# A linear-attention and expert kernel: key tiles in pairs, with copies and sums first, y steps from a list, and block sums on GpSimd

## The chip, the cores and the metric

The kernel runs on one core of one Trainium2 chip. The time is device microseconds of one execution, from launch to end as the device reports it; the median of several runs is given, and one further execution was recorded by the profiler. Engines carry the profile's names: PE (TensorE matmul) and PEld (its weight load), DVE (VectorE), ACT (ScalarE), POOL (GpSimd), and SP, which here only issues DMAs.

## The reference

For 2048 tokens of width 512 the reference mixes an attention block without softmax and a mixture of eight experts, of which all eight are used:

```python
qkv = (x @ wqkv)                                  # 32 heads of 16
phi = lambda t: where(t > 0, t + 1, exp(t)) + 1e-6
kv  = einsum("bhsd,bhse->bhde", phi(k), v)
z   = einsum("bhsd->bhd", phi(k))
a   = (phi(q) @ kv / (phi(q) @ z + 1e-6)) @ wo
logits = x @ w_gate                               # 8 experts, top 8
b   = sum over e of softmax(logits)[e] * (silu(x @ w1[e]) @ w2[e])
g   = sigmoid(sum(x * gate_w))
out = g * a + (1 - g) * b
```

All of it is in float32.

## The kernel before

Each float32 operand is split into a high part in the rounded format fp32r and a low part with the remainder, and each product is made of three matmuls (high by high, high by low, low by high: `mm3`, lines 59 to 62). A split is a copy by ACT and a subtraction by DVE (`split`, lines 350 to 352). Large products are done with a scheme of seven block products in place of eight (P1 to P7), for which sums and differences of blocks of the operands are needed.

The program has three stages, written out in the order in which each engine's queue takes the instructions; no scheduler changes that order. The first stage works on keys, the second and third on experts and queries. The change lies in the first, the function `keys`, up to about 130 us of the span.

Tokens are in four blocks of 512 (ORD = 2, 3, 0, 1), each of four tiles of 128. For blocks 2 and 3 `g_proj` makes the key projection of one tile directly, in two groups of columns (g = 0 and 1, 12 matmuls each), and `group_done` and `pk_done` put phi on it: ACT takes the exponential (line 74) and the relu (line 75) of the bank, DVE the minimum and sum (line 78), ACT the high part `pkh` (line 65, by the helper `act_copy`) and DVE the low part (line 88). GpSimd adds the tile into `pks` by an accumulating DMA (lines 472 and 477). `split_xt` splits the tokens by rows, and `y_acc` then adds x^T phi(k) of that tile to four banks that stay through the stage: 12 matmuls over 512 columns, or 6 for half of them with `part` 0 or 1.

Blocks 0 (A) and 1 (B) are done as pairs j = 0 to 3: tile j of A on top and tile j of B at the bottom. `x_sum` makes the sums of the token blocks (four steps for the keys, p = 0, and four for blocks 2 and 3, p = 1, which the experts use), `w_sums` those of the key weights, `x_part` and `w_part` split them. `pair` issues seven products into PSUM banks: product 0 into bank a; a copy of bank a goes into bank b (ACT, kb<-ka), on which product 2 is added; product 1 goes into bank c, which is copied to s3; product 3 is added to a, then copied to s2; product 4 is added to c, and DVE adds it to s2 (line 689); product 5 is added to a, and DVE adds it to s3 (line 696); product 6 is added to a. `late` keeps the second halves of phi until `flush` issues them. `more` lists what other work stands between the products (`extra(0)` to `extra(3)`), and the loop at lines 720 to 741 places the y steps of the tiles before. There is one bank b and one bank c, and there are two of a.

The SP queue issues the loads in program order: `load_xt` for rows of tokens (two rooms), `load_x` for columns (three rooms), and later the first expert weights (`m.load`).

Of the kernel before, what the change touches and what calls it, by code (L numbers as in the profile page):

```python
# [26 lines left out]
NTT = TB // P  # L27
# [5 lines left out]
HALF = 2 * P  # L33
# [290 lines left out]
def keys(m):  # L324
# [195 lines left out]
    def x_sum(p, step):  # L520
        a, b = raw[2 * p], raw[2 * p + 1]
        b11, b21, b12, b22 = a[:, :2], a[:, 2:], b[:, :2], b[:, 2:]
        dst, x, y = ((b11, b12, b11), (b12, b22, b12), (b22, b22, b11), (b21, b21, b22))[step]
        v.tensor_sub(dst, x, y)

    def x_part(p, i):
        a, b = raw[2 * p], raw[2 * p + 1]
# [26 lines left out]
            nc.sync.dma_start(w0[i], src[:, 2 * i:2 * i + 2, :HALF])  # L554

    def w_sums():
        v.tensor_add(w11, w10, w11)
        v.tensor_sub(w10, w00, w10)
        v.tensor_sub(w00, w11, w00)
        v.tensor_sub(w01, w01, w00)  # L560

    def w_part(i):
        src = {1: w11, 5: w10, 3: w00, 4: w01}[i]
# [33 lines left out]
    for t in range(NTT - 1):  # L597
# [4 lines left out]
    x_keep(0, (2, 0)), x_keep(2, (2, 1))  # L602


    A, B = ORD[2], ORD[3]
    beside = {
        0: (lambda: w_sums(), lambda: w_part(1), lambda: split_x(A, 0)),
        1: (lambda: split_x(A, 1), lambda: split_x(A, 2), lambda: split_x(A, 3), lambda: w_part(4)),
        2: (lambda: x_sum(0, 0), lambda: split_x(B, 2), lambda: split_x(B, 3), lambda: x_part(0, 1)),
        3: (lambda: x_sum(0, 1), lambda: x_sum(0, 2), lambda: x_part(0, 3)),  # L610
    }
    T1 = ORD[1] * NTT
    for t in range(NTT):
        for g in range(2):
            g_proj(T1 + t, g, alone=True)
        split_xt(T1 + t)
        y_acc(T1 + t - 1)
        for do in beside[t]:
            do()
        if t == 1:  # L620
            x_keep(4, (3, 1))
            load_xt(A)
            band(mask.rearrange("p (b e) -> p b e", e=DH), [[-DH, P // DH], [0, DH]], 1)
# [21 lines left out]

    late = []

    def flush():
        while late:
            late.pop(0)()  # L650

    def group(t, g, src, done):
        d = pk[t][0]
        if g == 0:
            act_copy(lg[:, t, :E + 2], src[:, HALF:W[0]])
        dst, src = d[:, HALF:] if g == 0 else d[:, :HALF], src[:, :HALF]
        m.phi_first(dst, src)
        late.append(lambda: m.phi_last(dst, src))
        if done:
            late.append(lambda: pk_done(t, False))  # L660


    def pair(j, extra):
        top, bot = A * NTT + j, B * NTT + j
        a = m.ps_tile(f"ka{j}", "a")
        product(j, 0, a, True)
        flush()
        b = m.ps_tile(f"kb{j}", "b")
        act_copy(b[:, :W[0]], a[:, :W[0]])
        yield  # L670
        c = m.ps_tile(f"kc{j}", "c")
        product(j, 1, c, True)
        s3 = oh_tile(f"k3_{j}")[:, :HALF]
        act_copy(s3, c[:, :HALF])
        yield
# [20 lines left out]
        v.tensor_add(s3, a[:, :HALF], s3)  # L696
        group(bot, 1, s3, True)
        yield
        product(j, 6, a, False)
        flush()  # L700
# [2 lines left out]
    def last_step(run):  # L703
        for _ in run:
            pass

    more = {
        0: ((lambda: w_part(3),), (lambda: w_part(5), lambda: x_part(0, 5)),
            (lambda: split_xt(4), lambda: x_sum(0, 3)), (lambda: x_part(0, 6), lambda: split_xt(0), lambda: load_x(3))),
        1: ((), (lambda: split_xt(5),), (lambda: x_sum(1, 0), lambda: x_part(1, 1)),  # L710
            (lambda: split_xt(1), lambda: x_sum(1, 1))),
        2: ((lambda: split_xt(6, True),), (lambda: x_part(1, 5), lambda: split_xt(2, True)),
            (lambda: x_sum(1, 2), lambda: split_xt(7, True)),
            (lambda: split_xt(3, True), lambda: m.load(0), lambda: m.load(1))),
        3: ((lambda: x_part(1, 3),), (lambda: x_sum(1, 3),), (lambda: x_part(1, 6),), (lambda: m.prep(0, 0),)),
    }

    old = None
    touch()
    for j in range(NTT):  # L720
        before = (B * NTT + j - 1, A * NTT + j - 1) if j else (T1 + NTT - 1, None)
# [11 lines left out]
        next(run)  # L733
        y_acc(before[0], 1)
        next(run)
        if j and j < NTT - 1:
            y_acc(before[1], 0)
        next(run)
        if j:
            y_acc(before[1], 1 if j < NTT - 1 else None)  # L740
# [746 lines left out]
```

## Time and profile before

| | |
|---|---|
| Median of 3 runs | 2351.36 us (2350.36 to 2353.77) |
| The profiled execution, its own time | 2351.11 us |
| Its span, first to last instruction | 2349.4 us |
| Busy: PE, DVE, ACT, POOL | 2320.7, 1835.6, 1416.9, 158.0 us |
| Mean granted TensorE clock | 0.993 of full speed |

All rows of the profile count from the start of the span. A row of the timeline gives start, duration, engine, line, operation, the output and input names and, in brackets, how long the engine stood idle before and what released it. Starts on one engine can overlap the end of the instruction before, since engines pipeline. Waits are listed as total, number of times and longest.

### The profile page before, as it was taken

Reading aid. Unit: us, or ns where it says so; the run is one execution under the profiler, and the core shown is the slowest. Engines: PE = TensorE matmul, PEld = TensorE weight load, DVE = VectorE, ACT = ScalarE, POOL = GpSimd, SP = SyncE. Lnnn points to the kernel's source line nnn. Section 1 sums busy time; section 2 is a strip of 40 time slices with the busy share of each in tenths; the row PEclk is TensorE's granted clock in tenths of the full one; section 3 lists DMA queues with packets and bytes.
Section 4 is the critical chain, followed back from the end, with each engine's and each line's share of the span. In section 5 each row is a group of like instructions: output and inputs, shape, how many; then the busy total and the mean of one; then the engine's idle time right before and its main releaser. Section 6 shows DMA issues by size and latency. Waiting matters only on the chain.

```text
span 2349.4 us, 31599 instructions
## 1 busy us (share of the span) xinstructions
PE 2320.7 (99%) x10523; PEld 1924.3 (82%) x10523; DVE 1835.6 (78%) x3132; ACT 1416.9 (60%) x2686; POOL 158.0 (7%) x218
## 2 busy tenths in 40 slices
PE   9799999999999999999999999999999999999999
PEld 8678888888888888888888888888888888888887
DVE  6589888888888888888766868777677776867777
ACT  6477766666665666666555656555565655655553
POOL 1010100000000000000001000000011101000011
PEclk9899999999999999999999999999999999999999
DMA  8379888888889888888946444574556646466568
GB/s 273 110 245 308 286 269 257 273 265 270 273 259 282 260 265 268 272 281 250 318 156 174 150 157 161 171 206 139 161 175 184 184 148 179 153 175 174 162 213 234
DMA packets 323908, 513.42 MB, mean 219 GB/s; under 512 B 52176, under 2 KB 220512, under 8 KB 323104
## 3 DMA queue, kind: packets, MB, share of 16 engines
q1 hardware_dynamic: 294832, 465.14, 59.7%
q0 software_dynamic: 23200, 45.21, 11.0%
q8 instruction: 82, 1.34, 0.2%
q10 hardware_dynamic: 5712, 1.06, 0.2%
q14 instruction: 82, 0.67, 0.1%
HBM read 345.03 MB, written 163.13 MB: 216 GB/s over the span
## 4 chain that ended last, share of the span: by engine, by line
PE 95%; ACT 0%; DVE 0%; issue 0%
PE p L60 15%; PE p L62 15%; PE p L61 15%; PE a L60 9%; PE a L62 9%; PE a L61 9%; PE c L60 4%; PE c L62 4%; PE c L61 4%; PE b L62 2%; PE b L61 2%; PE b L60 2%; PE s L60 0%; PE s L62 0%; PE s L61 0%; PE y L60 0%
## 5 line engine op out<-in xcount | busy, mean ns | idle before, releaser
L60 PE MATMUL p<-ho,w 128*128 128x512 f32 x1602 | 623.3, 389 | 0.0
L62 PE MATMUL p<-ho,w 128*128 128x512 f32 x1602 | 623.2, 389 | 0.0
L61 PE MATMUL p<-ho,w 128*128 128x512 f32 x1602 | 623.2, 389 | 0.0
L959 DVE TENSOR_TENSOR ho<-s,ho 128x512 fp32r<-128x512 f32 x784 | 538.3, 687 | 39.4 <-ACT ho L65 36.8
L65 ACT ACTIVATE ho<-s 128x512 fp32r<-128x512 f32 x784 | 482.0, 622 | 16.6 <-PE p L62 10.8
L60 PEld LDWEIGHTS p<-ho,w 128*128 128x128 f32 x1602 | 300.8, 188 | 62.8 <-DMA w<-w2stash 0.5
L62 PEld LDWEIGHTS p<-ho,w 128*128 128x128 f32 x1602 | 300.8, 188 | 62.3
L61 PEld LDWEIGHTS p<-ho,w 128*128 128x128 f32 x1602 | 300.8, 188 | 62.3
L65 ACT ACTIVATE o<-rs 128x512 fp32r<-128x512 f32 x224 | 129.4, 578 | 203.0 <-PE c L62 113.6
L65 ACT ACTIVATE o<-rm 128x512 fp32r<-128x512 f32 x240 | 138.8, 578 | 144.0 <-PE a L62 66.0
L885 DVE TENSOR_TENSOR s<-c,s 128x512 f32<-128x512 f32 x116 | 80.2, 691 | 153.5 <-PE c L62 145.4
L65 ACT ACTIVATE ws<-rm 128x256 fp32r<-128x256 f32 (+1 forms) x204 | 114.9, 572 | 48.3 <-DMA w2stash<-ws 44.3
L797 ACT ACTIVATE s<-s 128x512 f32<-128x512 f32 x224 | 138.5, 618 | 6.2 <-DVE s L890 3.4
L797 ACT ACTIVATE s<-b 128x512 f32<-128x512 f32 x112 | 67.2, 600 | 103.3 <-PE b L62 98.0
L205 DVE TENSOR_TENSOR o<-rm,o 128x512 fp32r<-128x512 f32 x180 | 123.3, 685 | 1.3 <-ACT o L65 1.2
L65 ACT ACTIVATE s<-a 128x512 f32<-128x512 f32 x116 | 69.3, 597 | 89.4 <-PE a L62 89.3
L219 DVE TENSOR_TENSOR ws<-rm,ws 128x512 fp32r<-128x512 f32 x155 | 106.6, 688 | 17.2 <-ACT ws L65 16.2
L890 DVE TENSOR_TENSOR s<-a,s 128x512 f32<-128x512 f32 x116 | 79.8, 688 | 51.1 <-PE a L62 50.8
L205 DVE TENSOR_TENSOR o<-rs,o 128x512 fp32r<-128x512 f32 x168 | 114.4, 681 | 5.6 <-ACT o L65 5.6
L65 ACT ACTIVATE b<-a 128x512 f32<-128x512 f32 x116 | 67.2, 579 | 60.9 <-PE a L62 60.8
L1018 POOL DMA_DIRECT2D acct<-c x30 | 25.8, 859 | 914.4 <-DVE c L1012 747.7
L65 ACT ACTIVATE s<-c 128x512 f32<-128x512 f32 x116 | 68.9, 594 | 22.2 <-PE c L62 22.2
(371 smaller groups left out, 4581.6 us busy)
## 6 DMA issues: line engine op xcount, KB each, us to landing
w<-w2stash SPq DMA_DIRECT2D x403, 512.0 KB, 4.1
w2stash<-ws SPq DMA_DIRECT2D x359, 256.0 KB, 4.6
rm<-wm SPq DMA_DIRECT2D x228, 256.0 KB, 5.2
rs<-wm SPq DMA_DIRECT2D x108, 256.0 KB, 4.0
wb<-wgtd SPq DMA_DIRECT2D x16, 512.0 KB, 5.0
acct<-c POOLq DMA_DIRECT2D x30, 256.0 KB, 6.2
acct<-d POOLq DMA_DIRECT2D x30, 256.0 KB, 5.3
acct<-k POOLq DMA_DIRECT2D x30, 256.0 KB, 5.0
```

What stands on the lines that cost most here:

```text
L60: nc.tensor.matmul(ps, wh, xh, start=start, stop=False, skip_group_check=True)
L61: nc.tensor.matmul(ps, wh, xl, start=False, stop=False, skip_group_check=True)
L62: nc.tensor.matmul(ps, wlo, xh, start=False, stop=stop, skip_group_check=True)
L65: nc.scalar.activation(dst, src, AF.Copy, scale=scale, bias=bias)
L205: v.tensor_sub(two(o, 1), src, f32(two(o, 0)))
L219: v.tensor_sub(two(w, 1), src, f32(two(w, 0)))
L797: nc.scalar.activation(dst, src, AF.Silu)
L885: v.tensor_add(sn[g, 2], bank[g, "c"], sn[g, 2])
L890: v.tensor_add(sn[g, 3], bank[g, "a"], sn[g, 3])
L959: v.tensor_sub(h[1], s, f32(h[0]))
L1018: nc.gpsimd.dma_start(m.acct[part.h, j, dt], s, accum_op=ALU.add)
```

## The change

In `pair`, the copy of bank a to bank b and the other bank copies and sums now stand ahead of `flush` or right behind the product that they need, and `extra` is called at other places. The y steps are taken in halves from a list `behind`, to which each finished tile adds two; `y_next` takes one from its front. The token sums and the weight sums are done by GpSimd in place of VectorE, and the first of them, with two splits, are issued ahead of the tiles of block 3. The lists `beside` and `more` are dealt out anew.

```diff
     def x_sum(p, step):
...
-        v.tensor_sub(dst, x, y)
+        nc.gpsimd.tensor_sub(dst, x, y)
...
     def w_sums():
-        v.tensor_add(w11, w10, w11)
-        v.tensor_sub(w10, w00, w10)
-        v.tensor_sub(w00, w11, w00)
-        v.tensor_sub(w01, w01, w00)
+        nc.gpsimd.tensor_add(w11, w10, w11)
+        nc.gpsimd.tensor_sub(w10, w00, w10)
+        nc.gpsimd.tensor_sub(w00, w11, w00)
+        nc.gpsimd.tensor_sub(w01, w01, w00)
...
+    behind = []
+    def y_next():
+        if behind:
+            y_acc(*behind.pop(0))
     A, B = ORD[2], ORD[3]
+    split_x(A, 0), split_x(A, 1)
+    w_sums()
+    x_sum(0, 0), x_sum(0, 1)
     beside = {
-        0: (lambda: w_sums(), lambda: w_part(1), lambda: split_x(A, 0)),
-        1: (lambda: split_x(A, 1), lambda: split_x(A, 2), lambda: split_x(A, 3), lambda: w_part(4)),
-        2: (lambda: x_sum(0, 0), lambda: split_x(B, 2), lambda: split_x(B, 3), lambda: x_part(0, 1)),
-        3: (lambda: x_sum(0, 1), lambda: x_sum(0, 2), lambda: x_part(0, 3)),
+        0: (lambda: split_x(B, 2), lambda: split_x(B, 3), lambda: w_part(1)),
+        1: (lambda: x_sum(0, 2), lambda: split_x(A, 2), lambda: split_x(A, 3), lambda: w_part(4)),
+        2: (lambda: x_sum(0, 3), lambda: x_part(0, 1), lambda: w_part(3)),
+        3: (lambda: x_part(0, 3),),
     }
...
         split_xt(T1 + t)
-        y_acc(T1 + t - 1)
+        y_next() if t else y_acc(T0 + NTT - 1)
+        behind.extend(((T1 + t, 0), (T1 + t, 1)))
...
     def pair(j, extra):
         product(j, 0, a, True)
-        flush()
         b = m.ps_tile(f"kb{j}", "b")
         act_copy(b[:, :W[0]], a[:, :W[0]])
+        flush()
+        extra(0)
         yield
         product(j, 1, c, True)
         act_copy(s3, c[:, :HALF])
+        extra(1)
         yield
         product(j, 2, b, False)
-        extra(0)
...
         product(j, 3, a, False)
+        flush()
         act_copy(s2, a[:, :W[0]])
-        flush()
-        extra(1)
+        extra(2)
         yield
         product(j, 4, c, False)
-        extra(2)
         v.tensor_add(s2, c[:, :W[0]], s2)
...
         product(j, 5, a, False)
+        v.tensor_add(s3, a[:, :HALF], s3)
         flush()
+        group(bot, 1, s3, True)
         extra(3)
-        v.tensor_add(s3, a[:, :HALF], s3)
-        group(bot, 1, s3, True)
...
     more = {
-        0: ((lambda: w_part(3),), (lambda: w_part(5), lambda: x_part(0, 5)),
-            (lambda: split_xt(4), lambda: x_sum(0, 3)), (lambda: x_part(0, 6), lambda: split_xt(0), lambda: load_x(3))),
...
+        0: ((lambda: w_part(5), lambda: x_part(0, 5)), (lambda: split_xt(4), lambda: split_xt(0)), (lambda: x_part(0, 6),),
+            (lambda: load_x(3),)),
+        1: ((lambda: split_xt(5),), (lambda: split_xt(1),), (lambda: split_xt(6, True),),
+            (lambda: x_sum(1, 0), lambda: x_sum(1, 1), lambda: split_xt(2, True))),
+        2: ((lambda: split_xt(7, True), lambda: split_xt(3, True), lambda: m.load(0), lambda: m.load(1),
+             lambda: x_sum(1, 2)), (lambda: x_part(1, 1),), (lambda: x_sum(1, 3), lambda: x_part(1, 5)), ()),
+        3: ((lambda: x_part(1, 3),), (lambda: m.prep(0, 0),), (lambda: x_part(1, 6),), ()),
     }
...
         run = pair(j, extra)
-        for _ in range(3):
-            next(run)
+        next(run), next(run), y_next(), next(run)
         if old:
             last_step(old)
-        y_acc(before[0], 0)
...
+        y_next(), next(run), y_next(), next(run), next(run)
+        y_next()
         old = run
     last_step(old)
+    y_next()
     flush()
-    y_acc(B * NTT + NTT - 1)
     for k in range(1, 8):
         m.prep(0, k)
-    y_acc(A * NTT + NTT - 1)
+    while behind:
+        y_next()
```

More of the change, by code (lines that the diff above doesn't have):

```diff
@@ L646, in keys, with flush @@
     late = []
-    def flush():
-        while late:
+    def flush(n=None):
+        while late if n is None else n:
             late.pop(0)()
+            n = n and n - 1
     def group(t, g, src, done):
@@ L660, in group @@
             late.append(lambda: pk_done(t, False))
+            behind.extend(((t, 0), (t, 1)))
     def pair(j, extra):
@@ L707, in keys @@
     more = {
-        0: ((lambda: w_part(3),), (lambda: w_part(5), lambda: x_part(0, 5)),
-            (lambda: split_xt(4), lambda: x_sum(0, 3)), (lambda: x_part(0, 6), lambda: split_xt(0), lambda: load_x(3))),
[L710 to L715, printed above, removed]
+        0: ((lambda: w_part(5), lambda: x_part(0, 5)), (lambda: split_xt(4), lambda: split_xt(0)), (lambda: x_part(0, 6),),
[5 more added lines that the diff above has]
+        3: ((lambda: x_part(1, 3),), (lambda: m.prep(0, 0),), (lambda: x_part(1, 6),), ()),
     }
@@ L720, in keys @@
     for j in range(NTT):
-        before = (B * NTT + j - 1, A * NTT + j - 1) if j else (T1 + NTT - 1, None)
         def extra(i):
@@ L727, in keys @@
         run = pair(j, extra)
-        for _ in range(3):
-            next(run)
+        next(run), next(run), y_next(), next(run)
         if old:
             last_step(old)
-        y_acc(before[0], 0)
[L733 to L740, printed above, removed]
+        y_next(), next(run), y_next(), next(run), next(run)
+        y_next()
         old = run
     last_step(old)
+    y_next()
     flush()
-    y_acc(B * NTT + NTT - 1)
     for k in range(1, 8):
         m.prep(0, k)
-    y_acc(A * NTT + NTT - 1)
+    while behind:
+        y_next()
     m.ys = ys
```

## The prediction, made before the changed kernel had run

> **What bounds the kernel now.** I read the page's chain that ended last first (nearly all of it lies on PE, so time is won only where PE idles or runs slow), then the table of stretches around the one place where the granted clock falls, then TensorE's waits there, then the timeline of one pair. Columns of a stretch: bounds, length, busy time of PE, PEld, DVE, ACT, POOL, granted clock, DMA share.
>
> ```profile
> 52.10:58.90 6.80, 5.33 (x18) 4.75 (x19) 2.29 (x4) 2.88 (x7) 0.00 (x0) 0.51 0.99 316
> 69.10:76.00 6.90, 5.15 (x18) 4.67 (x19) 1.96 (x4) 2.90 (x9) 0.00 (x0) 0.52 0.00 0
> 86.20:93.00 6.80, 3.01 (x13) 3.02 (x14) 3.66 (x6) 3.29 (x9) 0.00 (x0) 0.52 0.00 0
> 106.70:110.10 3.40, 3.40 (x15) 3.12 (x15) 2.03 (x4) 2.32 (x6) 0.00 (x0) 0.53 0.60 226
> 120.30:127.20 6.90, 5.98 (x17) 4.29 (x16) 4.92 (x10) 2.83 (x7) 1.75 (x4) 0.52 0.17 47
> 48.00:130.40 82.40, 59.20 (x280) 50.44 (x280) 46.37 (x71) 37.52 (x86) 6.57 (x10) 0.81 0.42 127
> PE kb L60 <- ACT kb L65: 17.8, 4, 5.4
> PE ka L60 <- DVE k L696: 2.5, 1, 2.5
> ```
>
> In the stage of pairs (48.0 to 130.4) TensorE stands idle for 82.4 - 59.2 = 23.2 us. 17.8 of these are four waits of product 2 for the bank copy a to b. Each long wait is followed by a stretch at about half clock; PE is busy for 5.33 + 5.15 + 3.01 + 3.40 + 5.98 = 22.9 us in the five, of which half, 11.4, is lost. So idle time and slow clock together hold 34.6 us, and this is all that the change can win. Why the copy is late:
>
> ```profile
> 86.08 1.22 DVE L524 TENSOR_TENSOR x<-x 128x1024 f32<-128x1024 f32 x1
> 87.21 0.42 DVE L696 TENSOR_TENSOR k<-ka,k 128x256 f32<-128x256 f32 x1
> 88.11 0.42 ACT L75 ACTIVATE k<-k 128x256 f32<-128x256 f32 x1
> 88.56 0.43 DVE L78 SCALAR_TENSOR_TENSOR pk<-pk,k 128x256 f32<-128x256 f32 x1 [0.93 <-ACT k L75]
> 89.02 0.63 ACT L65 ACTIVATE pkh<-pk 128x512 fp32r<-128x512 f32 x1 [0.49 <-DVE pk L78]
> 89.56 0.37 ACT L65 ACTIVATE kb<-ka 128x266 f32<-128x266 f32 x1
> 89.69 0.69 DVE L88 SCALAR_TENSOR_TENSOR pkh<-pk,pkh 128x512 fp32r<-128x512 f32 x1 [0.70 <-ACT pkh L65]
> 89.99 0.59 PE L60 MATMUL kb<-g,x01h 128*128 128x266 f32 x1 [5.00 <-ACT kb L65]
> 82.90 0.28 PE L60 MATMUL ka<-g,x00h 128*128 128x266 f32 x1
> 83.01 0.29 PE L61 MATMUL ka<-g,x00h 128*128 128x266 f32 x1
> 45.53 0.40 PE L60 MATMUL y<-pkh,xt 128*128 128x512 f32 x1
> 130.38 0.23 PE b L821
> ```
>
> The copy at 89.56 stands on ACT behind pkh of the tile before, which waits for a chain on DVE that begins behind a sum of tokens (L524). TensorE has by then been idle for 5.00 us.
>
> **What PE still has to do after 45.5.** A product's matmul starts 0.12 us after the one before (82.90 to 83.01), so six take 0.72. A full y step (12 matmuls of 512) takes 2.74: 45.53 to the touch matmul at 48.27, shown below. The last g_proj ends at 45.53 before; in the changed order y_next stands at this place. From there the changed order has 11 full y steps (half steps put off by the list are in these) and 28 products: 11 x 2.74 + 28 x 0.72 + 0.1 = 50.4 us. The old one has 10 y steps, 47.7; with 34.6 lost this gives 82.3 of the 84.85 us up to 130.38, so some 2.5 us go in the ramps behind five stalls, 0.5 each.
>
> **Copies and halves.** With kb's copy ahead of flush it waits only for product 0, and between product 1 and product 2 stands a half y step, 1.37 us. In a steady pair PE then needs 7 x 0.72 + 4 x 1.37 = 10.5 us. ACT's items of such a pair (row durations of the fences here, starts 0.1 closer) are some 6.6 us, DVE's about 6, and each wait has a filler over it: kb's copy (0.37) under 1.37 us, pkh of the lower tile under two products and a half step. I cost pairs 1 to 3 at no wait; what covers is the half steps, and without them the four waits of 2.5 to 5.4 us return. The tail likewise: from the end of product 5 the last sum, exp, relu, minimum, pkh and its low half (0.42 + 0.42 + 0.42 + 0.43 + 0.63 + 0.69 = 3.0) lie under product 6 and two half steps, 3.46.
>
> **Sums on GpSimd: the queue.** Twelve sums leave DVE: 8 x 1.22 + 4 x 0.68 = 12.5 us. On POOL they stand in order behind and between the accumulating DMAs into pks, each of which waits for the one before to land:
>
> ```profile
> 38.92 0.84 POOL L472 DMA_DIRECT2D pks<-pk  x1 [6.24 <-DVE xt L352]
> 42.66 0.86 POOL L472 DMA_DIRECT2D pks<-pk  x1 [2.89 <-DMA pks<-pk]
> 47.51 0.34 POOL L452 TENSOR_SCALAR_AFFINE_SELECT mask<-mask 128x128 f32<-128x128 f32 x1
> 50.07 0.87 POOL L472 DMA_DIRECT2D pks<-pk  x1 [1.81 <-DVE xt L352]
> 60.53 0.86 POOL L472 DMA_DIRECT2D pks<-pk  x1 [9.59 <-DMA pks<-pk]
> 126.45 1.03 POOL L751 TENSOR_SCALAR_AFFINE_SELECT ident<-ident 128x128 f32<-128x128 f32 x2
> 31.81 0.68 DVE L557 TENSOR_TENSOR r<-r,r 128x512 f32<-128x512 f32 x1
> ```
>
> The row at 38.92 is the fourth pks DMA; w_sums come fifth, so they start at 38.92 + 0.84 = 39.8, not at 31.81. No row shows a sum on POOL. Lower ends are DVE's 0.68 (512 elements) and 1.22 (1024). Upper ends scale the one-input select of 128 elements, 0.515 at 126.45: 2.06 and 4.1. I take the middle, 1.4 and 2.6, since nothing speaks for either end. The Trainium skill's GPSIMD Engine Reference, section Elementwise — side-by-side cycle accounting, gives 4497 ns for 2048 elements, so by an estimate 2.25 us for 1024 and 1.15 for 512; the sum below would then give 2330, and no run here shows it yet.
>
> **Where ACT waits for that.** w_part(1) is on ACT's in-order queue ahead of tile T1+1, and everything of that tile is queued behind it:
>
> ```profile
> 32.53 0.64 ACT L65 ACTIVATE wide<-r 128x512 fp32r<-128x512 f32 x1 [1.31 <-DVE r L557]
> 39.85 0.17 ACT L65 ACTIVATE lg<-g 128x10 f32<-128x10 f32 x1
> 40.86 0.75 DVE L78 SCALAR_TENSOR_TENSOR pk<-pk,g 128x256 f32<-128x256 f32 x2
> 41.64 0.63 ACT L65 ACTIVATE pkh<-pk 128x512 fp32r<-128x512 f32 x1 [0.52 <-DVE pk L78]
> 42.18 0.62 ACT L65 ACTIVATE xt<-xr 128x512 fp32r<-128x512 f32 x1
> 42.70 1.14 ACT L65 ACTIVATE x11h<-x 128x512 fp32r<-128x512 f32 x2
> 48.27 0.28 PE L642 MATMUL kb<-g,x00h 128*128 128x266 f32 x1
> 49.78 0.38 SPq L441 DMA_DIRECT2D xr<-x  x1
> 52.18 1.06 ACT L65 ACTIVATE t3h<-x 128x1024 fp32r<-128x1024 f32 x1 [3.23 <-DVE x L524]
> 53.14 0.38 ACT L65 ACTIVATE kb<-ka 128x266 f32<-128x266 f32 x1
> 53.57 0.59 PE L60 MATMUL kb<-g,x01h 128*128 128x266 f32 x1 [3.54 <-ACT kb L65]
> 65.25 1.04 ACT L65 ACTIVATE t6h<-x 128x1024 fp32r<-128x1024 f32 x1
> 66.33 1.23 DVE L352 TENSOR_TENSOR t6l<-x,t6h 128x1024 fp32r<-128x1024 f32 x1 [0.52 <-ACT t6h L65]
> ```
>
> One tile's round on ACT takes 2.85 (39.85 to 42.70), a split 0.52 more, lg to the end of the minimum 1.76.
> - wide ran at 32.53; now it needs the first sum, 39.8 + 1.4 = 41.2. PE meanwhile runs the tiles and half steps that don't need T1+1, to about 40, and waits for the banks of T1+1 until about 42.6 (wide, exp, relu and the minimum behind 41.2). It then still ends T1+3's tiles near 45.5, since a full y step was put off; a half clock there would fall inside the next wait.
> - 41.2 + 0.52 + 2.85, two splits 1.04, wide 0.65 (its sum done at 45.4), 2.85, t1h 0.96, wsum 0.52, 1.76: the minimum of T1+3 ends at 52.3. Then bank b is free and the touch matmul runs, at 52.3 instead of 48.27. PE has its half step to 46.9: **wait 1, 5.4 us**, with half clock after it as in the first row of all (53.57 to 58.90, 5.33 us, costs 2.67).
> - On POOL four w_sums end at 45.4, two token sums at 50.6, the fifth pks DMA starts, the sixth 3.74 later (38.92 to 42.66), 54.3; x_sum(0, 2) runs 55.2 to 57.8. t3h (1.06) waits for it on ACT, and kb's copy (0.38) stands behind t3h: 59.2. PE has touch, two products and a half step, at half clock for 5.33 us, to 57.9: **wait 2, 1.3**.
> - The seventh pks DMA waits for the sixth to land. Beside the loads of xr (49.78) and x this took 10.46 (50.07 to 60.53); these loads are now issued at about 54.4 (the xt split of T1+3, the last reader of their room, comes about 2 us behind the minimum at 52.3), so I take 10.46 and not 3.74: 64.8. x_sum(0, 3) 65.6 to 68.2, t6h 1.04, t6l 1.23, the sum on c 0.42: bank c is free at 70.9. PE reaches product 1 of pair 1 at 59.2 + 5 x 0.72 + 3 x 1.37 = 66.9: **wait 3, 4.0**, and a mean clock loss of 11.4 / 5 = 2.3.
> - x_sum(1, ...) each have most of a pair's 10.5 us ahead of the split that reads them; load_x(3) now waits for POOL instead of DVE, a pair ahead of use; the loads of the first weights now go ahead of the stash writes on SP, used in pair 3. All at nothing, covered by these pairs.
>
> **The sum.** 50.4 + waits 10.7 + clock 5.0 + ramps 1.5 = 67.6; 45.5 + 67.6 = 113.1 against 130.38: 17.3 us won. The experts behind run off PE's progress, so the gain stays. The profiled execution took 2351.1 (span 2349.4), the median of the runs is 2351.4: 2351.1 - 17.3 = 2333.8, say 2334. With the lower prices (touch 51.6, waits 2 and 3 gone, clock 2.7, ramps 0.5) it ends at 103.8: 2324.5. With the upper ones (waits 8.45, 5.45 and 1.8, clock 5.0, ramps 2.0) at 118.6: 2339. A change below 0.2%, 4.7 us, can't be told from none.
>
> **Rivals.**
> 1. *DVE and POOL take turns.* If a sum on POOL and a DVE subtraction of two tiles in SBUF can't run together, the six POOL sums between 39.8 and 52.3 (10.8 us) and DVE's ten such operations there (nine of 0.69, one of 1.23: 7.4 us) add up: wait 1 grows by 7.4, and the third token sum by about 1.6 more: 2343. For it: the selects took 0.515 at 126.45, beside DVE's subtractions, and 0.34 at 47.51. Against: DVE kept its pace then, and none of these was long. The Trainium skill's SBUF — State Buffer, section Who interferes with whom, has this rule: a VectorE instruction with two SBUF inputs and a GpSimd one that reads SBUF exclude each other for the whole instruction. The drawn-out select agrees in part. Chance 0.27.
> 2. *POOL's sums become the bound (slower).* wait 2 lies behind four weight and three token sums, worth five token sums. Beyond 4.1 us each microsecond of a token sum costs five, so from 4.1 + 12 / 5 = 6.5 us on the gain is gone; at 8.2, twice the upper end, 2339 + 20.5 = 2359. For it: no row shows such a sum. Against: 0.34 for 128 elements. Chance 0.08.
> 3. *Pairs keep a wait each.* The rounds of ACT and DVE, in order, may not fit 10.5 us: a wait of about 2.5 us (the smaller of the old ones) with its 2.3 of clock in each of pairs 1 to 3 takes 14: 2348, about no change. Against it stand 6.6 of 10.5 us on ACT. Chance 0.10.
>
> **How the numbers follow.** Forecast 0.55, rivals 0.27, 0.08, 0.10. The range 2324 to 2347 takes in both ends of the sums' prices and rival 1, and leaves out rival 2 and the most of rival 3. Faster: 0.54 + 0.25 + 0.05 = 0.84; the same: 0.07 (rest of rivals 1 and 3); slower: 0.09.
>
> **What would show it.** Right: POOL's first sum near 39.8, wide on ACT behind it; touch near 52; kb waits of pairs 1 to 3 gone; b at L821 (old line) near 113; half-clock stretches down from five to two or three. Wrong: a POOL sum over 4.1 us, DVE subtractions ending together with POOL's sums (rival 1), a wait of PE for ACT in every pair (rival 3).

## The result and the profile after

| | before | after |
|---|---|---|
| Median, 11 runs each | 2351.60 us (2350.36 to 2354.38) | 2345.70 us (2344.69 to 2347.10) |
| Ratio after to before, 95% interval | | 0.9974 (0.9964 to 0.9983) |
| The profiled execution, its span | 2351.11, 2349.4 us | 2345.95, 2344.2 us |
| End of the stage (first expert matmul, line 821, now 824) | 130.38 us | 123.71 us |

The change is faster by 5.9 us, about a third of the 17.3 that were forecast; the time lies in the range given, near its slow end, where the first rival (VectorE and GpSimd take turns, 2343) had put it.

First, TensorE's waits from 20 us to the end of the stage of pairs (total, times, longest):

```profile
PE kb L653 <- DVE pk L78: 10.4, 1, 10.4
PE g L491 <- DVE pk L78: 3.3, 1, 3.3
PE y L60 <- ACT pkh L65: 3.2, 2, 3.0
PE ka L60 <- ACT k L65: 2.1, 1, 2.1
PE kc L60 <- DVE k L702: 1.7, 1, 1.7
```

The touch matmul in the timeline, and the end of the stage in the chain that ended last:

```profile
60.30 0.59 PE L653 MATMUL kb<-g,x00h 128*128 128x266 f32 x1 [10.41 <-DVE pk L78]
```

```profile
123.71 0.23 PE b L824
```

The stretch of the whole stage (columns as for the kernel before: PE, PEld, DVE, ACT, POOL, clock, DMA share):

```profile
48.00:123.80 75.80, 57.77 (x303) 49.03 (x302) 54.76 (x73) 38.24 (x91) 27.39 (x22) 0.89 0.47 142
```

The four waits for the bank copy (17.8 us) are gone altogether. In their place stands one wait of 10.4 us ahead of the touch matmul, which runs at 60.30 where 52.3 was forecast and 48.27 was measured before, and shorter ones. DVE is busier than before (54.76 us in a stage of 75.8, against 46.37 in one of 82.4) though sums were taken from it. The timeline of POOL, ACT and DVE around that wait tells why:

```profile
39.34 1.58 POOL L557 TENSOR_TENSOR r<-r,r 128x512 f32<-128x512 f32 x1
40.95 0.63 ACT L65 ACTIVATE wide<-r 128x512 fp32r<-128x512 f32 x1 [8.82 <-POOL r L557]
41.00 1.26 POOL L558 TENSOR_TENSOR r<-w,r 128x512 f32<-128x512 f32 x1
41.62 1.20 DVE L352 TENSOR_TENSOR wide<-r,wide 128x512 fp32r<-128x512 f32 x1 [8.64 <-ACT wide L65]
42.74 0.74 DVE L78 SCALAR_TENSOR_TENSOR pk<-pk,g 128x256 f32<-128x256 f32 x2
44.17 1.68 DVE L88 SCALAR_TENSOR_TENSOR pkh<-pk,pkh 128x512 fp32r<-128x512 f32 x1 [0.70 <-ACT pkh L65]
45.27 2.83 POOL L524 TENSOR_TENSOR x<-x,x 128x1024 f32<-128x1024 f32 x1
45.78 2.86 DVE L352 TENSOR_TENSOR xt<-xr,xt 128x512 fp32r<-128x512 f32 x1
48.17 2.69 POOL L524 TENSOR_TENSOR x<-x 128x1024 f32<-128x1024 f32 x1
48.56 3.45 DVE L352 TENSOR_TENSOR x01l<-x,x01h 128x512 fp32r<-128x512 f32 x2
53.98 0.69 DVE L88 SCALAR_TENSOR_TENSOR pkh<-pk,pkh 128x512 fp32r<-128x512 f32 x1 [0.70 <-ACT pkh L65]
55.11 2.67 POOL L524 TENSOR_TENSOR x<-x,x 128x1024 f32<-128x1024 f32 x1
55.44 3.43 DVE L352 TENSOR_TENSOR t1l<-x,t1h 128x1024 fp32r<-128x1024 f32 x1 [0.17 <-ACT t1h L65]
```

Read it in pairs of rows. The subtraction xt starts at 45.78 inside the sum of 45.27, which ends at 48.10; xt, 0.69 us by itself, ends at 48.64, half a microsecond behind that end. The next pair of subtractions (1.29 by themselves) takes 3.45, t1l (1.23) takes 3.43: each ends only after the sum beside it. The five rows of drawn-out subtractions (wide, pkh at 44.17, xt, x01l, t1l; six operations) last 12.62 us in place of the 4.6 that they take alone, 8.0 more. Between two sums, at 53.98, a subtraction takes its 0.69 again. Phi's minimum (line 78 from bank g, which lies in PSUM) keeps its 0.42 or less beside a sum (42.74).

### The profile page after: what moved, and what is told of

Read it like the earlier page. It is cut to its first block, busy times and chain, and to the rows that moved or that the text cites. A ratio compares the mean times of both kernels' runs of the same rounds, so it can differ in the third digit from the quotient of the medians.

```text
span 2344.2 us, 31598 instructions
## 1 busy us (share of the span) xinstructions
PE 2316.6 (99%) x10523; PEld 1920.6 (82%) x10523; DVE 1838.6 (78%) x3120; ACT 1414.0 (60%) x2686; POOL 184.3 (8%) x230
## 4 chain that ended last, share of the span: by engine, by line
PE 94%; DVE 0%; DMA 0%; ACT 0%; SPq 0%; issue 0%; ACTq 0%
PE p L60 15%; PE p L61 15%; PE p L62 15%; PE a L60 9%; PE a L61 9%; PE a L62 9%; PE c L60 4%; PE c L62 4%; PE c L61 4%; PE b L61 2%; PE b L62 2%; PE b L60 2%; DMA w<-w2stash 0%; PE s L60 0%; PE s L62 0%; PE s L61 0%
## 5 line engine op out<-in xcount | busy, mean ns | idle before, releaser
L219 DVE TENSOR_TENSOR ws<-rm,ws 128x512 fp32r<-128x512 f32 x155 | 106.3, 686 | 16.6 <-ACT ws L65 15.9
```

Of the source, the lines that this page charges most:

```text
L219: v.tensor_sub(two(w, 1), src, f32(two(w, 0)))
```

## The experiments

Each was run in turn with the kernel before, on the same chip. The gain is the median of the kernel before, as it ran beside it, minus the kernel's own; by the intervals a gain is known to some 2 to 4 us, so that differences of 1 or 2 us between two kernels are hints only.

| label | what it is | median us | ratio, 95% interval | gain us |
|---|---|---|---|---|
| after | the changed kernel | 2345.7 | 0.9974 (0.9964 to 0.9983) | 5.9 |
| e1_dve | all 12 sums on VectorE | 2329.1 | 0.9905 (0.9890 to 0.9919) | 22.0 |
| e2_wpool | weight sums alone on GpSimd | 2336.4 | 0.9936 (0.9919 to 0.9952) | 14.7 |
| e3_xpool | token sums alone on GpSimd | 2334.5 | 0.9930 (0.9915 to 0.9945) | 16.6 |
| e4_bpool | before, its sums on GpSimd | 2372.6 | 1.0089 (1.0074 to 1.0104) | -21.4 |
| f1_write | short writes for the sums | 2330.2 | 0.9912 (0.9898 to 0.9927) | 20.5 |
| f2_one | one-input copies for the sums | 2333.1 | 0.9925 (0.9909 to 0.9942) | 17.6 |
| f3_wearly | e2, weight sums earlier | 2331.2 | 0.9919 (0.9905 to 0.9934) | 19.5 |
| f4_loads | e1, loads and row splits later | 2330.5 | 0.9914 (0.9899 to 0.9929) | 20.2 |
| g1_len | writes as long as the sums | 2338.0 | 0.9945 (0.9929 to 0.9962) | 13.6 |
| g2_flush | e1, copy behind flush again | 2330.2 | 0.9910 (0.9896 to 0.9925) | 21.5 |
| g3_fill | e1, one half y step earlier | 2336.1 | 0.9935 (0.9920 to 0.9950) | 15.6 |
| g4_copy | before, copy ahead of flush | 2345.4 | 0.9975 (0.9965 to 0.9985) | 6.3 |
| h1_loads | e1, weight loads later still | 2328.6 | 0.9902 (0.9887 to 0.9917) | 22.6 |
| h2_aload | after, weight loads later still | 2344.9 | 0.9972 (0.9961 to 0.9983) | 6.3 |
| h3_late | after, late token sums on VectorE | 2342.8 | 0.9962 (0.9950 to 0.9975) | 8.4 |
| h4_nofill | e1, no half y step ahead of product 2 | 2331.1 | 0.9914 (0.9899 to 0.9929) | 20.1 |
| i1_both | e1 with g2's and h4's edits | 2332.7 | 0.9920 (0.9903 to 0.9936) | 19.6 |
| i2_deal | e1, early sums dealt as before | 2331.2 | 0.9913 (0.9898 to 0.9927) | 21.1 |

### Sums back on VectorE: all, the tokens', the weights'; and GpSimd in the kernel before

```diff
# e1_dve: both; e2_wpool: x_sum only; e3_xpool: w_sums only
-        nc.gpsimd.tensor_sub(dst, x, y)      # x_sum
+        v.tensor_sub(dst, x, y)
-        nc.gpsimd.tensor_add(w11, w10, w11)  # w_sums, and three more
+        v.tensor_add(w11, w10, w11)
# e4_bpool: the same lines of the kernel before, the other way round
```

e1_dve:

> The changed kernel with all twelve sums given back to DVE; order of products, copies, fillers and loads as changed. Three theories of why 6 us were won and not 17. 'Turns': POOL's sums and DVE's operations on two SBUF tiles exclude each other. 'Queue': POOL's place behind the pks DMAs and its price, as in the forecast, only larger. 'Order': the new order on ACT and SP (early xt splits behind a late load, stash writes behind the first weights) takes it back, whoever makes the sums. Turns and queue both expect the touch matmul near 49 and about 2325 us; order expects more than 2338. No DVE subtraction of 512 elements should be longer than 0.7 us.

e2_wpool:

> The changed kernel with only the four weight sums on POOL, the eight token sums on DVE. Both turns and queue keep ACT's wait of about 9 us for the first weight sum behind the fourth pks DMA (wide at about 41). Queue: touch near 53, 2327 us. Turns: the DVE operations between 39 and 45 are drawn out by some 3 us in all, touch near 55, 2330 us. After 46 no drawn-out DVE operation under either.

e3_xpool:

> The changed kernel with only the eight token sums on POOL, the four weight sums on DVE. ACT's wait at wide goes. Queue: 2326 us. Turns: each token sum of 2.7 us holds up one or two DVE operations, some 4 us before the touch and, by the three sums in pairs 1 and 2, a wait of PE of about 3 us with slow clock after it: 2334 us. DVE operations of two SBUF tiles of 512 elements up to 3.4 us long beside the sums.

e4_bpool:

> The kernel before with the twelve sums on POOL and nothing else changed. The weight sums then stand behind the fifth pks DMA (42.66 before), so wide can run only at about 45 and ACT stands from 31 on. Queue: some 20 us slower than before, 2372 us. Turns: the drawn-out DVE operations come on top, 2380 us or more. If sums on POOL were a gain by themselves, it would be at or under 2351.

With all sums on VectorE the kernel wins 22.0 us, and the move to GpSimd gives 16.1 of these back (22.0 - 5.9). So the theory "order", which expected more than 2338, falls; the 2325 of the other two was missed by 4. The weight sums alone cost 7.3, the token sums alone 5.4, both together more than their sum. In the kernel before the same move costs 21.4. The first sums and the touch matmul in e1_dve's timeline, and two of TensorE's waits in it:

```profile
27.74 0.68 DVE L557 TENSOR_TENSOR r<-r,r 128x512 f32<-128x512 f32 x1
30.52 1.22 DVE L524 TENSOR_TENSOR x<-x,x 128x1024 f32<-128x1024 f32 x1
...
49.46 0.59 PE L653 MATMUL kb<-g,x00h 128*128 128x266 f32 x1 [3.96 <-DVE pk L78]
```

```profile
PE kc L60 <- DVE k L702: 2.9, 1, 2.9
PE ka L60 <- ACT k L65: 1.0, 2, 0.8
```

On VectorE the sums begin at 27.74 instead of 39.34, since they stand behind no accumulating DMA; the touch matmul runs at 49.46. From e3_xpool's groups (busy, then mean ns of one), and its first token sum in the timeline:

```profile
L352 DVE TENSOR_TENSOR xt<-xr,xt 128x512 fp32r<-128x512 f32 x11 | 14.3, 1316 | 1.5 <-ACT xt L65 1.5
```

```profile
39.22 2.73 POOL L524 TENSOR_TENSOR x<-x,x 128x1024 f32<-128x1024 f32 x1
```

xt's subtraction takes 1316 ns in the mean here; in e1_dve the same group has 686. The sums on GpSimd start near 39 here too, behind the fourth accumulating DMA.

Three of these expectations need a word. e2_wpool (2336.4) is slower than either theory allowed: touch came at 56.04, and only 1.5 us of that are drawn-out operations. VectorE's own two token sums, 1.2 us each, now stood ahead of touch in the late stretch as well (46.78 and 52.37). e3_xpool met the 2334 of the turns theory by luck: touch came at 47.77, earlier than in e1_dve, so nothing was lost ahead of it on balance; the loss lies behind it (first expert matmul at 112.42, against 106.81). e4_bpool came out at the queue theory's 2372, although there, too, subtractions of 0.69 us were drawn out (line 88 to 3.47 at 56.04). Times alone don't tell the theories apart here; the durations do.

### Is it the reading, or the length and the place? Writes and copies in the sums' stead

The length of the sums and their late place in GpSimd's queue could have cost all of it without any turn being taken. f1_write and g1_len leave the sums out and write a constant, reading nothing; f2_one leaves them out and copies their first operand.

```diff
# f1_write: one write; g1_len: three writes in a row; f2_one: one copy
-        nc.gpsimd.tensor_sub(dst, x, y)
+        nc.gpsimd.memset(dst, 0.05)      # f1_write; three times in g1_len
+        nc.gpsimd.tensor_copy(dst, x)    # f2_one
# and so for the four weight sums
```

f1_write:

> Each of the twelve GpSimd sums of the changed kernel is replaced by a GpSimd operation that writes a constant into the same destination and reads nothing (the sums are left out of the computation). All GpSimd queue places and all waits on the results stay. Theory A, DVE and POOL take turns because both READ SBUF: the DVE subtractions beside the POOL operations go back to 0.69 us (512 elements) and 1.23 (1024), none above 1.5 us, and the time lies near the sums-on-VectorE run plus the queue part: 2329 to 2337. Theory B, turns are taken for any POOL access, writes too: DVE subtractions beside the writes still last as long as these (over 2 us where a write of 1024 elements takes that long), 2338 to 2346. Theory C, no contention but the queue place alone cost the 16.6 us: touch stays near 60 us and the time is at 2343 or more with DVE at 0.69 and 1.23.

f2_one:

> Each of the twelve GpSimd sums of the changed kernel is replaced by a GpSimd copy of its first operand (one SBUF input in place of two; the sums are left out of the computation). Theory A, any POOL operation that reads SBUF excludes a DVE operation with two SBUF inputs for its whole length: DVE subtractions beside the copies end together with them, with durations of up to 1.2 us plus the length of the copy; if a copy takes as long as a sum (2.7 us for 1024 elements) the time stays near 2346, if it takes half of it, near 2337. Theory B, only two-input POOL operations exclude DVE: DVE keeps 0.69 and 1.23 us, 2329 to 2335.

g1_len:

> Each of the twelve GpSimd sums of the changed kernel is replaced by three writes of a constant into its destination, which read nothing but together take about as long as the sum (3 x 0.46 = 1.4 us for 512 elements, 3 x 0.9 = 2.7 us for 1024); the sums are left out of the computation. GpSimd's queue and the times at which its results are ready stay nearly as in the changed kernel, only the reads of SBUF are gone. Turns theory: this is the kernel that the prediction reckoned with, touch at 52 to 53 us, VectorE subtractions at 0.69 and 1.23 us, 2331 to 2336, and the 10 to 14 us up to 2345.7 are what the turns cost. Rival, the length of the sums and their place behind the accumulating DMAs cost most of it: touch at 57 or later, 2339 to 2345 although VectorE runs at full pace.

The timeline of f1_write at its first token blocks:

```profile
41.29 2.16 POOL L524 MEMSET x<- 128x1024 f32 x2
43.27 0.69 DVE L88 SCALAR_TENSOR_TENSOR pkh<-pk,pkh 128x512 fp32r<-128x512 f32 x1 [0.70 <-ACT pkh L65]
```

That of f2_one at the same place:

```profile
42.39 2.49 POOL L524 COPY x<-x 128x1024 f32<-128x1024 f32 x2
42.92 1.06 DVE L88 SCALAR_TENSOR_TENSOR pkh<-pk,pkh 128x512 fp32r<-128x512 f32 x1 [0.70 <-ACT pkh L65]
43.90 1.52 DVE L352 TENSOR_TENSOR xt<-xr,xt 128x512 fp32r<-128x512 f32 x1
```

And that of g1_len, with TensorE's two waits behind it:

```profile
45.82 5.89 POOL L525 MEMSET x<- 128x1024 f32 x6
48.89 0.69 DVE L88 SCALAR_TENSOR_TENSOR pkh<-pk,pkh 128x512 fp32r<-128x512 f32 x1 [0.70 <-ACT pkh L65]
49.50 0.68 DVE L352 TENSOR_TENSOR xt<-xr,xt 128x512 fp32r<-128x512 f32 x1
52.90 0.39 PE L658 MATMUL kb<-g,x00h 128*128 128x266 f32 x1 [4.05 <-DVE pk L78]
60.61 0.59 PE L60 MATMUL kb<-g,x01h 128*128 128x266 f32 x1 [2.92 <-ACT kb L65]
```

Beside 5.89 us of writes DVE keeps 0.69 and 0.68; beside copies of 1.24 each, xt takes 1.52. By its time alone f2_one (2333.1) would have fitted the theory that only two-input operations hold DVE up; its rows decide. So it is GpSimd's reading of SBUF that holds DVE up, with one input or two, and its writing does not. The Trainium skill's SBUF — State Buffer, section Who interferes with whom, says it so: a VectorE instruction with two SBUF inputs and a GpSimd one that reads SBUF shut each other out for a whole instruction; these three runs and the changed kernel agree, to the length (0.69 beside writes, up to 2.9 beside a sum of 2.8).

g1_len splits the loss. Its writes are on POOL for as long as the sums (5.84 us for the first two token blocks, against 5.5), so results come as late as in the changed kernel, but nothing is read. It wins 13.6 us. From 22.0 to 13.6, **8.4 us, is the length and the place of the sums** in GpSimd's queue; from 13.6 to 5.9, **7.7 us, are the turns** (each of the two by some 4 us either way). The expectation of 2331 to 2336 was missed by 2 us, between the two theories' ranges. The stage's ends say the same: touch 49.46, 52.90, 60.30 in e1_dve, g1_len and the changed kernel, and the start of the first expert matmul in the timeline 106.81, 116.13, 123.55. From touch to that matmul both g1_len and the changed kernel take 63.2 us, so on balance the 7.4 us that the turns add to the stage lie ahead of touch.

The 8.4 us are net of the work that the sums no longer are on VectorE. Of them the place by itself is the small part: f1_write, with the same place in the queue and writes that hold it for 0.5 or 0.9 us each, still wins 20.5, 1.5 less than e1_dve, which is within the uncertainty. It is length in a late place that costs.

### The place alone: weight sums earlier on GpSimd

```diff
# f3_wearly, against e2_wpool
+    w_load()                    # ahead of block 2's tiles
     for t in range(NTT):
         split_xt(T0 + t)
         g_proj(T0 + t, 1, ...)
+        if t == 1:
+            w_sums()            # removed further down
```

> The kernel with only the four weight sums on GpSimd (2336.4 us), with their loads moved ahead and the sums issued behind the second tile of block 2, so ahead of the third accumulating DMA on GpSimd's queue, near 24 to 30 us of the span. Theory Q, the 7.3 us that the weight sums cost lie in their place in the GpSimd queue, which makes ACT's in-order queue wait some 9 us for the split wide: the wait goes, the touch matmul comes at 49 to 50 us and the time is 2328 to 2331. Theory T, turns of DVE and GpSimd alone cost them: they are then taken with the tiles of block 2 instead, DVE operations of 0.69 us beside the sums last 1.2 to 2 us, touch stays at 53 or later and the time is 2333 to 2337.

It lies at the border of the two: the gain goes from 14.7 to 19.5. The run that was profiled was the slowest of its four (2334.4; the others 2330.6 to 2331.2), so its late times are no measure. Its timeline on DVE, POOL and PE:

```profile
24.05 4.34 DVE L352 TENSOR_TENSOR x30l<-x,x30h 128x512 fp32r<-128x512 f32 x2
24.52 1.64 POOL L557 TENSOR_TENSOR r<-r,r 128x512 f32<-128x512 f32 x1
28.45 0.39 PE L491 MATMUL g<-g,x30l 128*128 128x266 f32 x1 [1.04 <-DVE x30l L352]
53.97 0.59 PE L654 MATMUL kb<-g,x00h 128*128 128x266 f32 x1 [2.59 <-DVE pk L78]
```

ACT's wait for the split wide is gone, as the queue theory wants, but the turns have moved with the sums: two subtractions of block 3 take 4.34 us (1.29 in e1_dve), and TensorE now waits for them one microsecond at a time. GpSimd's sums look cheaper in this place, and not as cheap as on VectorE (22.0), though both differences are about as large as the uncertainty.

### The late sums, and the waits that were costed at nothing

```diff
# h3_late, against the changed kernel
-        nc.gpsimd.tensor_sub(dst, x, y)
+        (v if p else nc.gpsimd).tensor_sub(dst, x, y)
# h1_loads (against e1_dve) and h2_aload (against the changed kernel)
-        2: ((..., lambda: m.load(0), lambda: m.load(1), lambda: x_sum(1, 2)), (lambda: x_part(1, 1),),
-            (lambda: x_sum(1, 3), lambda: x_part(1, 5)), ()),
+        2: ((..., lambda: x_sum(1, 2)), (lambda: x_part(1, 1),),
+            (lambda: x_sum(1, 3), lambda: x_part(1, 5), lambda: m.load(0), lambda: m.load(1)), ()),
# f4_loads (against e1_dve): both loads behind x_part(1, 1); split_xt(4), split_xt(0) to more[0][2] and [0][3]
```

h3_late:

> The changed kernel (2345.7 us) with the four late token sums (the blocks for the experts, issued in pairs 1 and 2) on VectorE and the eight early sums on GpSimd. If the turns of pairs 1 and 2 cost what TensorE's waits there say (some 3 us for pkh, 2.1 for bank a and the half clock behind them): 2339 to 2342. If only the early ones count, as the rival in the prediction reckoned: 2344.5 to 2346.5.

h1_loads:

> The changed kernel with all twelve sums on VectorE (2329.1 us), the two first expert weight loads moved on SP's queue from ahead of the first stash writes to behind the second ones. Theory, the loads ahead of the stash writes cause the wait of ACT's split for the stash (3.1 us) and TensorE's 2.9 us for bank c: both waits go or fall under 1 us, stage end 103 to 104 in place of 106.8, 2325 to 2327. Rival, the writes themselves take as long as a pair allows: the wait stays at one of the later splits, 2328 to 2330.

h2_aload:

> The changed kernel as it is, sums on GpSimd (2345.7 us), with the same move of the two weight loads behind the second stash writes. Theory: the stash wait of 3.9 us on ACT goes and with it TensorE's 1.7 us for bank c, 2342 to 2345. Rival, the turns of VectorE and GpSimd in that pair are late anyway: 2345 to 2347.

f4_loads:

> The changed kernel with all twelve sums on VectorE (2329.1 us), the first two expert weight loads moved behind the split of the sum that writes the stash (so the stash writes go first on SP), and the two row splits of pair 0 moved behind the copy of bank a to s2. Theory: the wait for the stash (3.1 us on ACT, then 2.9 us of PE for bank c) and the wait for the rows xr (3.6 us on ACT, 1.0 of PE for bank a) come from these two places, which the prediction costed at nothing. Both go: stage end near 103 to 104 instead of 107.0, 2325 to 2327. Rival: the loads only move the wait to pair 3, where the first weights are used later than planned, 2329 or slower.

In the changed kernel three sums in a row hold up phi itself in pair 2, since line 78 there reads its exponential and the bank's copy k from SBUF (timeline of the changed kernel; beside the sum of the last row VectorE is idle):

```profile
83.84 2.72 POOL L524 TENSOR_TENSOR x<-x,x 128x1024 f32<-128x1024 f32 x1
84.96 1.89 DVE L78 SCALAR_TENSOR_TENSOR pk<-pk,k 128x256 f32<-128x256 f32 x1 [0.36 <-ACT k L75]
86.64 2.47 POOL L524 TENSOR_TENSOR x<-x 128x1024 f32<-128x1024 f32 x1
86.78 2.89 DVE L352 TENSOR_TENSOR xt<-xr,xt 128x512 fp32r<-128x512 f32 x1
89.19 2.67 POOL L524 TENSOR_TENSOR x<-x,x 128x1024 f32<-128x1024 f32 x1
89.59 2.56 DVE L78 SCALAR_TENSOR_TENSOR pk<-pk,k 128x256 f32<-128x256 f32 x1
92.86 0.80 PE L60 MATMUL y<-pkh,xt 128*128 128x512 f32 x1 [3.05 <-ACT pkh L65]
100.00 2.69 POOL L524 TENSOR_TENSOR x<-x,x 128x1024 f32<-128x1024 f32 x1
```

In h3_late the wait at 92.86 is gone, but bank c waits 2.6 where it waited 1.7 and bank a 3.4 where it waited 2.1. The gain grows from 5.9 to 8.4, to 2342.8: between the two expected ranges, and the intervals overlap, so that the late sums cost some 2.5 us is a hint. In h3_late they leave GpSimd altogether, so their length and their turns are not told apart.

The stash wait was real but not what held up the end. h1_loads takes away ACT's wait for the stash (3.1 us in e1_dve), and TensorE's waits only change places (rows of h1_loads):

```profile
PE ka L60 <- ACT k L65: 1.8, 2, 1.0
PE ka L60 <- DVE k L707: 1.1, 1, 1.1
PE kc L60 <- DVE k L702: 0.7, 1, 0.7
```

Bank c's 2.9 fell to 0.7 and bank a's 1.0 rose to 2.9. The gains of h1_loads, h2_aload and f4_loads can't be told from those of the kernels they start from: the theory of these three fell. In f4_loads the wait had merely gone to a later split, since two loads still stood ahead of the second stash writes.

### What won the 22 us: copies first, fillers, early sums

```diff
# g2_flush, against e1_dve
-        act_copy(b[:, :W[0]], a[:, :W[0]])
         flush()
+        act_copy(b[:, :W[0]], a[:, :W[0]])
# g4_copy: the same two lines of the kernel before, the other way round
# h4_nofill, against e1_dve; i1_both: this and g2_flush's edit
-        next(run), next(run), y_next(), next(run)
+        next(run), next(run), next(run), y_next()
# g3_fill, against e1_dve
+    y_next()
     touch()
# i2_deal, against e1_dve: the lists beside and more[0] of the kernel before, and
-    split_x(A, 0), split_x(A, 1)
-    w_sums()
-    x_sum(0, 0), x_sum(0, 1)
```

g2_flush:

> The changed kernel with all twelve sums on VectorE (2329.1 us), and in each pair the copy of bank a to bank b behind flush again, as in the kernel before; the list of half y steps stays. Theory, the order of the copy is what removed the four waits of product 2: the waits for the copy return in pairs 1 to 3, 2 to 5 us each with half clock behind them, 2338 to 2348. Rival, the half y step from the list, which now stands between product 1 and product 2, covers the late copy: waits under 1 us, 2329 to 2333.

g4_copy:

> The kernel before with one edit: in each pair the copy of bank a to bank b stands ahead of flush. The y steps and all sums stay as they were. Theory, the copies alone: of 17.8 us of waits for the copy in four pairs those of pairs 1 to 3 (14.3) shrink to under 1 us each, with most of the half clock behind them, and 10 to 20 us are won, 2331 to 2341. Rival, without a filler between product 1 and product 2 the chain on ACT is late for the next user (the tile's phi, the y steps or bank c), and less than 5 us are won, 2346 to 2351.

h4_nofill:

> The changed kernel with all twelve sums on VectorE (2329.1 us), and the half y step between product 1 and product 2 moved behind product 2; the copy of bank a to bank b stays ahead of flush. Theory, the half step is what covers the copy: TensorE waits for the copy again in pairs 0 to 3, 0.5 to 1.5 us each, with half clock only where a wait is long, 2331 to 2336. Rival, the copy ahead of flush needs no cover: waits under 0.3 us and 2328 to 2330.

i1_both:

> The changed kernel with all twelve sums on VectorE (2329.1 us), with both the copy of bank a to bank b behind flush again and the half y step between products 1 and 2 moved behind product 2. Theory, the two cover for one another: each undone alone cost 1 to 2 us, both together bring back waits for the copy of 2 us or more in three or four pairs with half clock behind them, 2337 to 2347. Rival, they are not what won: 2331 to 2334.

i2_deal:

> The changed kernel with all twelve sums on VectorE (2329.1 us), but the sums and splits of the tiles of block 3 and of pair 0 dealt out as in the kernel before (nothing ahead of block 3's tiles); the pairs' order, the list of half y steps and the dealing of pairs 1 to 3 stay as changed. Theory, the early dealing only matters for pair 0: its waits of the kernel before (3.5 us for the copy, and for t3h and t6h behind their sums on VectorE) return, 2331 to 2336. Rival, the early dealing is the most of the win: 2338 or more. Second rival, it is worth nothing: 2328 to 2330.

g3_fill:

> The changed kernel with all twelve sums on VectorE (2329.1 us), and one more half y step taken from the list ahead of the touch matmul. It fills 1.4 of the 4.0 us that TensorE waits there (3.96 to about 2.6), and the list runs one half shorter behind it. Theory: 2327 to 2328.5, less by up to 1.7 more if the 3.4 us at half clock behind the wait go too. Rival: the last half y step of pair 0 then meets a tile whose high part is not done, and the wait only moves: 2329 to 2331.

TensorE's waits for the bank copy: the first row is g4_copy's, the second g2_flush's, the third i1_both's (h4_nofill has 0.6 us in two waits):

```profile
PE kb L60 <- ACT kb L65: 14.4, 4, 4.3
```

```profile
PE kb L60 <- ACT kb L65: 2.0, 3, 1.3
```

```profile
PE kb L60 <- ACT kb L65: 6.6, 3, 2.7
```

In the kernel before, the copy ahead of flush takes only 3.4 of 17.8 us off the waits (6.3 us of time, between the two expected ranges): the copy is then late for what else stands ahead of it on ACT. In pair 0 that is the split t3h, which waits 3.2 us for VectorE's token sum. In pairs 1 to 3 it is phi of the pair before, whose exponential waits for the sum into s3 on VectorE (line 696; 5.3 us in four waits). ACT in g4_copy:

```profile
85.40 0.42 ACT L74 ACTIVATE pk<-k 128x256 f32<-128x256 f32 x1 [2.23 <-DVE k L696]
86.17 0.37 ACT L65 ACTIVATE kb<-ka 128x266 f32<-128x266 f32 x1
```

The change also moved this sum, to stand right behind its product, and in e1_dve ACT has no wait for it; what that move is worth alone was not tried. In e1_dve, on the other hand, neither the copy's place nor the half y step is missed when it alone is undone; undone together (i1_both) 6.6 us of waits return, yet the gain falls only from 22.0 to 19.6, since bank c's wait falls from 2.9 to 0.2 and half clock follows only one of the three waits. Copy and half step cover for one another, as the prediction had it, but they are not the win by themselves. Nor is the early dealing of pair 0's sums (i2_deal, 21.1).

g3_fill was slower than either theory allowed. Its waits:

```profile
PE y L60 <- ACT pkh L65: 6.5, 4, 2.4
PE kb L653 <- DVE pk L78: 2.6, 1, 2.6
```

The wait ahead of touch shrank from 4.0 to 2.6 as reckoned; but the later y steps come one half earlier, and four of them meet a tile whose high part is not done, 6.5 us where e1_dve has 0.2. One half step less of lead in the list costs some 6 us, the half clock behind two of these waits included. So the win needs the list's lead: that much the runs show. How much of the 22 us the lead as a whole, the dealing of pairs 1 to 3 and the other bank copies and sums moved in `pair` each make was not taken apart and stays open.

## Why the prediction was right and wrong, by its steps

- **What bounds the kernel**: right. The waits for the copy and the slow clock behind them could be won; e1_dve won 22.0 of the 34.6 us, and the four waits were gone in it as in the changed kernel.
- **Copies and halves, pairs at no wait**: nearly right for the design, for half a reason. The bank copy waits nowhere in e1_dve; that without the half steps "the four waits of 2.5 to 5.4 us return" was not borne out: h4_nofill has 0.6 us of them. Pairs 1 to 3 were not at no wait either (2.9 us for bank c and 0.8 for bank a in e1_dve).
- **Sums on GpSimd, the queue**: right. Start 39.34 (39.8 reckoned), 1.26 to 1.60 us for 512 elements (1.4), 2.47 to 2.83 for 1024 (2.6), wide at 40.95 (41.2).
- **Wait 1**: the step that failed. With the touch matmul at 52.3 and a wait of 5.4 the prediction took DVE's subtractions at 0.69 and 1.23 beside the sums, so that the two engines' work overlapped at no cost. They took 8.0 us more, touch came at 60.30, and the wait was 10.4. Rival 1's sum had 7.4 for it and 59.7. That the step was sound but for this, g1_len shows: without reads touch came at 52.90.
- **The choice of case**: "DVE kept its pace then, and none of these was long" was the reason to give the turns 0.27. It rested on a select of 0.515 us; its stretching was seen and put down as agreeing "in part". The rule that was cited beside it held, and it weighed more than that row.
- **Rival 1's size**: 2343 against 2345.7. It counted the sums up to the touch and the third token sum. The late sums of pairs 1 and 2 take turns as well (a wait of 3.05 at 92.86); h3_late puts some 2.5 us on them, length and turns together. That the result came so near 2343 is in part luck, since the waits behind touch were mis-sized too.
- **Waits 2 and 3**: 1.3 and 4.0 were reckoned. In g1_len, the kernel that the forecast described, the chain behind them held (rows of tokens loaded at 54.87, seventh accumulating DMA at 65.24, bank c free near 71.9; 54.4, 64.8 and 70.9 were reckoned), and they were 2.92 and, at bank c, 1.79; a wait of 3.2 for bank c in pair 3 came on top, behind a wait of ACT of 3.8 for the stash. So it ended at 116.13, not 113.1, and at 2338.0, not 2334. Of the 11.7 us between forecast and result the turns are thus 7.7 and the sizes of the later waits the rest, 4.0.
- **The clock**: 5.0 was reckoned. The changed kernel has three stretches at half clock (0.51 from 44.2 to 47.6, 0.54 from 53.5 to 63.8, 0.50 from 92.0 to 98.8), in which PE is busy for 3.40, 3.50 and 5.94 us; half of that, 6.4, is lost. Five had been there before, and two or three were forecast.
- **"All at nothing"**: wrong as a statement on waits. ACT waited 3.9 us for the stash, and the late token sums brought TensorE's wait of 3.05, with half clock behind it. In time the stash alone can't be told from nothing (h2_aload, h1_loads). ACT's wait of 6.0 us for rows of tokens, whose load was issued at 64.19, stood in no term.
- **The sign of the GpSimd edit**: the prediction bounded what the sums on GpSimd cost, but set it against nothing: with them on VectorE the same reordering would have been worth 22. It never asked where VectorE had time to spare. In e1_dve the first six sums run from 27.74 to 33; they put the low part of the tile's phi off from 30.48 (changed kernel) to 34.36, and touch still came at 49.46, 1.2 us later than in the kernel before. The sums that "leave DVE" were little burden there.

## What to carry to other kernels

Before work is moved from VectorE to GpSimd to relieve it, see whether VectorE's operations beside it read two operands from SBUF: here they waited for the end of each GpSimd operation that reads SBUF, so one of 0.69 us took up to 2.89 in the changed kernel. Look also for what is queued ahead of the work on GpSimd, and for a stretch on VectorE in which it would cost little. And when a filler is taken from a list of finished work, keep the list's lead: one half step less of it cost 6 us here.

## What the runs showed of the hardware that was not expected

- How far a short VectorE operation is stretched: 0.69 to 2.89 us beside a GpSimd sum of 2.5 to 2.8 (3.47 in e4_bpool, at 56.04), 0.69 to 1.78 beside one-input copies of 1.2 to 1.4, and not at all beside GpSimd writes of the same total length as the sums.
- Phi's minimum kept its pace when one of its inputs lay in PSUM (0.74 for two at 42.74, beside a sum) and was stretched from 0.42 to 2.56 when both lay in SBUF (89.59, beside the sum of 89.19).
- GpSimd's own sums were not drawn out: with VectorE idle they took 1.58 us (39.34) and 2.69 (100.00), beside its subtractions 1.26 to 1.60 and 2.47 to 2.83. It was VectorE that waited. One of f2_one's copies shows the other way round: 1.12 us at 40.65, beside a subtraction that kept its 0.69, where two others took 0.61.
- Whether half clock followed a wait of TensorE of about 2 us did not go by the wait's length. In g3_fill it followed waits of 1.59 and 1.85 us (a clock of 0.57 from 66.0 to 70.0 and 0.54 from 96.6 to 100.2) and not one of 2.42 (1.00 from 81.0 to 84.4); in i1_both it did not follow one of 2.13 (1.00 from 93.0 to 96.4).
